# The last expert's weight in column halves, with the first output groups written by halves

## The chip, the core and the metric

The kernel runs on one core of one Trainium2 chip. The metric is the device time of one execution in microseconds, as the median of several runs. The kernel before takes 160.81 us (three runs, 159.79 to 162.02). The core has a matrix engine (TensorE, "PE" in the profile), a vector engine (VectorE, "DVE"), a scalar engine (ScalarE, "ACT"), GpSimd ("POOL"), and SyncE ("SP"), which in this kernel issues the output transfers. Sixteen DMA engines move data between memory and the core's SBUF.

## The reference, cut to what matters

Two operators run one after the other. The first is an attention in which each query sees six chunks of 32 keys, chosen by an upper bound on the chunk's scores; 4 batches, 8 heads, 768 positions, 64 columns a head. Its output, as a matrix x of 3072 rows and 512 columns, feeds a soft mixture of eight experts with four slots each:

```python
logits = x @ phi                       # 3072 x 32
d = softmax(logits, axis=0)            # over the rows
slot_input = (d.T @ x).reshape(8, 4, 512)
for e in range(8):
    h = np.maximum(slot_input[e] @ w1[e], 0.0)   # 4 x 1024
    slot_out[e] = h @ w2[e]                      # 4 x 512
c = softmax(logits, axis=1)            # over the slots
out = c @ slot_out.reshape(32, 512)    # 3072 x 512
```

Every row of the output needs every slot's output, so no row can be finished before the last expert's w2 has been used. But a column of the output needs only that column of each w2.

## The kernel before, in words

**The attention** works on 16 pairs of heads, p = 0 to 15, in one loop written out by hand (the schedule is manual: each engine runs its instructions in the order of the code). For each pair there are six units of scores (`UNITS`). `scores(p, u)` lets TensorE make the scores in PSUM and ScalarE take the exponential into an SBUF tile `ex`. `select(p, u)`, on GpSimd, sets the part above the diagonal of units 0 to 3 to zero, in place in `ex` (line 339). `pv_mm(p, u)` multiplies `ex` by the values (line 353); within a unit the block on the diagonal comes last. The units of one pair are spread over the loop: the products of units 0 and 1 come at the end of the pair's own turn, the others in the next turn.

**The loads** of keys, queries, values and weights are all issued from GpSimd's queue[...]. `load_w(i)` for i = 0 to 7 brings `w1` of an expert (line 115), for i = 8 to 15 its `w2` (line 121). The list `w_at` says in which turn which of them is issued; the last two, `w2` of experts 6 and 7, are issued at the end of the turn of pair 13. In GpSimd's order the next instructions are the four selections of pair 14, then the making of a small constant (`stack`), then the selections of pair 15. In the profile the tiles of `w2` are called w_0_97 to w_7_104, and the last one, w_7_104, is what the change is about. It is loaded in three pieces: the first four of its eight row groups (`to[:, 0]`, line 124), then two pieces of two groups each (line 127).

**After the last pair** TensorE sums up the slots (`slot_first`, `slot_last`), makes `h` for both groups of four experts (`h_mm`, line 692), transposes it (`turn_h`), and sums `h @ w2` into two PSUM tiles `so_ps[0]` and `so_ps[1]`, one for each half of 256 columns (`so_mm`, line 724): first experts 0 to 3, then 4 to 6 with the first half of the columns before the second, then expert 7 in the three pieces in which its weight lands. Each `so_mm` of expert 7 covers both halves of the columns.

**The output.** The two sums are copied to `so` in bf16 (lines 743 and 744, VectorE and ScalarE). Then 12 groups of 256 rows follow: two products each (`o_ps`, line 756), copied out by VectorE and ScalarE (line 757) to a tile `o_sb`, and sent by SyncE (lines 759 and 761). In the first group each row tile is sent alone; the others go out as 512 KB with 4 KB a partition. After the second group, `turn_c` and `take_c` (lines 763 and 764) prepare the weights `cT` of the last batch.

Of the kernel before, what the change touches and what calls it, by code (L numbers as in the profile page):

```python
# [9 lines left out]
F32 = mybir.dt.float32  # L10
BF16 = mybir.dt.bfloat16
# [19 lines left out]
def kernel(  # L31
# [10 lines left out]
    nc = tc.nc  # L42
    B, H, S, D = q.shape
# [3 lines left out]
    P = 128  # L47
    NT = S // P
# [5 lines left out]
    Dm, NS = moe_phi.shape  # L54
    E, _, F = moe_w1.shape
    SPE = NS // E
    NDG = Dm // P
    NFG = F // P
    FH = F // 2
    GH = FH // P  # L60
# [50 lines left out]
    w2_sb = [static.tile([P, NFG, Dm], BF16, name=f"w2_{e}") for e in range(E)]  # L111

    def load_w(i):
        if i < E:
            nc.gpsimd.dma_start(out=w1_sb[i], in_=moe_w1[i].rearrange("(g p) f -> p g f", p=P))
        else:

            to = w2_sb[i - E].rearrange("p (n g) d -> p n (g d)", n=2)
            rows = moe_w2[i - E].rearrange("(n p g) d -> p n (g d)", n=2, p=P)
            if i < 2 * E - 1:  # L120
                nc.gpsimd.dma_start(out=to, in_=rows)
            else:

                nc.gpsimd.dma_start(out=to[:, 0], in_=rows[:, 0])
                for c in range(0, GH * Dm, GH * Dm // 2):
                    z = c + GH * Dm // 2
                    nc.gpsimd.dma_start(out=to[:, 1, c:z], in_=rows[:, 1, c:z])

    load_k(0)
    load_q(0)  # L130
# [4 lines left out]
        out=ident, in_=ident, compare_op=ALU.not_equal, fill=1.0,  # L135
# [22 lines left out]
        out=ahead, in_=ahead, compare_op=ALU.is_ge, fill=NEG,  # L158
# [38 lines left out]
    cT = static.tile([P, B * S], BF16, name="cT")  # L197
# [259 lines left out]
    def turn_c(b, pool, tag):  # L457

        c = st.pop(("c", b))
        ps = pool.tile([P, NT, P], BF16, name="cT_ps", tag=tag)  # L460
        for t in range(NT):
            for g in range(2):
                nc.tensor.matmul(
                    ps[g * 2 * NS:(g + 1) * 2 * NS, t, :], lhsT=c[:, t], rhs=ident, is_transpose=True)
        st["cps", b] = ps

    def take_c(b):

        ps = st.pop(("cps", b)).rearrange("s (g t) (j i a) -> s t g i a j", t=2, i=2, a=PP)
        to = cT[:, b * S:(b + 1) * S].rearrange("s (g i t a j) -> s t g i a j", i=2, t=2, a=PP, j=NJ // 2)  # L470
        for t in range(2):
            nc.scalar.copy(to[:, t], ps[:, t])
# [16 lines left out]
    for j in range(NJ):  # L489
        for i in range(2):  # L490
            nc.tensor.matmul(
                k0_ps[j // (NJ // 2)][i * D:(i + 1) * D, j % (NJ // 2), :], lhsT=src[:, i, j, :],
                rhs=ident[:NP, :NP], is_transpose=True)
# [24 lines left out]
    bounds_min(1)  # L518
    blocks(1, nc.vector.tensor_mul)
    load_w(0)  # L520
    load_k(4)
    relu_q(1, lambda to, x: nc.gpsimd.tensor_scalar_max(to, x, 0.0))
# [6 lines left out]
    for p in range(NPAIR):  # L529
# [42 lines left out]
        if p == 0:  # L572
            load_w(1)
# [54 lines left out]
        for i in w_at[p]:  # L628
            load_w(i)
        if p == NPAIR - 2:  # L630
# [7 lines left out]
            for g in range(4):  # L638
                nc.gpsimd.affine_select(
                    out=stack, in_=stack, compare_op=ALU.not_equal, fill=1.0,  # L640
                    base=-g * NS, pattern=[[-1, NS]], channel_multiplier=1)
            e_all = static.tile([P, NS], F32, name="e_all")
            hT = [h_all[:, i] for i in range(2)]
# [6 lines left out]
    halves = ((0, NT // 2), (NT // 2, NT))  # L650
# [25 lines left out]
    moe = ctx.enter_context(tc.tile_pool(name="moe", bufs=2, reuse_waits="tile"))  # L676
    outp = ctx.enter_context(tc.tile_pool(name="outp", bufs=7, reuse_waits="tile"))
    ps_h = ctx.enter_context(tc.tile_pool(name="ps_h", bufs=4, space=bass.MemoryType.PSUM, reuse_waits="tile"))
    ps_o = ctx.enter_context(tc.tile_pool(name="ps_o", bufs=4, space=bass.MemoryType.PSUM, reuse_waits="tile"))
# [5 lines left out]
    DH = Dm // 2  # L685
# [17 lines left out]
    def turn_h(eg, f):  # L703
        h_sb = st["h", eg, f]
        hT_ps = ps_o.tile([P, GH, P + NS], BF16, name="hT_ps", tag="o")
        for fg in range(GH):
            nc.tensor.matmul(
                hT_ps[:, fg, :P], lhsT=h_sb.rearrange("p (c g) -> p g c", g=GH)[:, fg, :], rhs=ident, is_transpose=True)

        c = 4 * SPE * eg  # L710

        def own_slots(t):
            return t[:, :, c:c + 4 * step].rearrange("p f (g s) -> p f g s", s=step)[:, :, :, :SPE]

        nc.vector.tensor_copy(own_slots(hT[eg][:, f * GH:(f + 1) * GH]), own_slots(hT_ps))

    def so_mm(experts, rows, spread=False):

        units = [(e, fg, i) for i in range(2) for fg in rows for e in experts]
        if not spread:  # L720
            units = [(e, fg, i) for fg in rows for i in range(2) for e in experts]
        for n, (e, fg, i) in enumerate(units):
            g = n % 4
            nc.tensor.matmul(
                so_ps[i][32 * g:32 * (g + 1), :], lhsT=hT[e // 4][:, fg, 32 * (e % 4):32 * (e % 4 + 1)],
                rhs=w2_sb[e][:, fg, i * DH:(i + 1) * DH],
                start=(e < 4 and fg == 0), stop=(e == E - 1 and fg == NFG - 1), skip_group_check=True)

    h_mm(0, 0)
    h_mm(0, 1)  # L730
# [3 lines left out]
    turn_h(0, 1)  # L734
    turn_h(1, 0)
    so_ps = [ps_o.tile([P, DH], F32, name=f"so_ps{i}", tag="o") for i in range(2)]
    so_mm(range(4), range(NFG))
    turn_h(1, 1)
    so_mm(range(4, E - 1), range(NFG), True)
    for a, z in ((0, GH), (GH, GH + GH // 2), (GH + GH // 2, NFG)):  # L740
        so_mm((E - 1,), range(a, z), True)
    so = moe.tile([P, Dm], BF16, name="so")
    nc.vector.tensor_copy(so[:, :DH], so_ps[0])
    nc.scalar.copy(so[:, DH:], so_ps[1])


    for g in range(B * NT // 2):
        rows = out[2 * g * P:2 * (g + 1) * P, :].rearrange("(p i) d -> p i d", i=2)
        o_sb = outp.tile([P, 2, Dm], F32, name="o_sb", tag="o_sb")
        for i in range(2):  # L750
            n = 2 * g + i

            cuts = (0, DH, Dm) if n == 0 else (0, Dm)
            for m, (a, z) in enumerate(zip(cuts, cuts[1:])):
                o_ps = ps_o.tile([P, z - a], F32, name="o_ps", tag="o")
                nc.tensor.matmul(o_ps, lhsT=cT[:, n * P:(n + 1) * P], rhs=so[:, a:z])
                (nc.vector.tensor_copy if (i + m) % 2 == 0 else nc.scalar.copy)(o_sb[:, i, a:z], o_ps)  # L757
            if g == 0:
                nc.sync.dma_start(out=rows[:, i], in_=o_sb[:, i])
        if g > 0:  # L760
            nc.sync.dma_start(out=rows, in_=o_sb)
        if g == 1:
            turn_c(B - 1, ps_h, "h")
            take_c(B - 1)


# [28 lines left out]
```

The softmax here doesn't subtract the row's maximum and nothing guards it: scores larger than these inputs give would overflow.

## Time and profile before

| | |
|---|---|
| median, lowest and highest of 3 runs | 160.81, 159.79, 162.02 us |
| span of the profiled execution | 159.6 us |
| busy share of PE, DVE, ACT, POOL | 88%, 72%, 69%, 61% |
| mean granted clock of TensorE | 0.963 |
| loads (GpSimd's queue) | 26.25 MB as stored, in bf16 |
| output (SyncE's queue) | 6.29 MB |
| attention and slots on TensorE, up to | 130 us |
| h and the experts' sums | 130 to 140.2 us |
| output stream on the DMA engines | from about 142 to 158 us |

A line of the timeline reads: start in us, duration in us, engine, line of the code, operation, output and inputs; in square brackets stands how long the engine was idle before it, and what ended the wait. In the table of DMA issues the last column is the time from issue to landing. "PEclk" is the clock that TensorE was granted, in tenths of full speed.

### The profile page before, as it was taken

The page shows a single profiled execution, that of the slowest core. Times are in us where ns is not written, and L with a number is a line of the kernel's source. Part 1 is how long each engine was busy: PE and PEld are TensorE (multiplying, and loading weights), DVE is VectorE, ACT ScalarE, POOL GpSimd, SP SyncE. Part 2 cuts the span into 40 slices and gives each one's busy share as a digit, 9 for nine tenths or more (in the row PEclk, how much of TensorE's full clock was granted, in tenths as well). Part 3 has the DMA queues.
Part 4 walks back from the last instruction along what each step waited for, and adds up shares of the span by engine and source line. Part 5 has one row for each costly group of instructions (what it writes and reads, how often), then busy time and mean ns, then how long its engine had stood idle before and what let it go on. Part 6 is the DMA issues. An engine that isn't in the chain of part 4 may idle for free.

```text
span 159.6 us, 6240 instructions
## 1 busy us (share of the span) xinstructions
PE 140.3 (88%) x2644; PEld 92.5 (58%) x2644; DVE 114.5 (72%) x366; ACT 110.4 (69%) x145; POOL 97.2 (61%) x177
## 2 busy tenths in 40 slices
PE   6869889999999999999999999999999999878200
PEld 2346566767767776766767667665755866632000
DVE  3966987889898778998898698889449444069400
ACT  3256967789888877989896978979879522079300
POOL 6978799597878959597786859677656001000000
PEclk9986999999999999999999999999999999999955
DMA  2999999999999999999999999999999999439996
GB/s 38 158 179 193 210 193 209 184 183 163 191 188 210 196 207 195 211 193 208 199 185 208 198 211 196 209 197 215 205 206 215 215 215 210 87 118 407 404 408 241
DMA packets 40475, 32.93 MB, mean 206 GB/s; under 512 B 26368, under 2 KB 32512, under 8 KB 40448
## 3 DMA queue, kind: packets, MB, share of 16 engines
q0 software_dynamic: 38576, 26.25, 111.2%
q1 hardware_dynamic: 1872, 6.29, 10.0%
q8 instruction: 20, 0.33, 0.7%
q14 instruction: 7, 0.06, 0.1%
HBM read 52.49 MB, written 6.29 MB: 368 GB/s over the span
## 4 chain that ended last, share of the span: by engine, by line
PE 40%; DMA 28%; POOL 13%; issue 5%; ACT 3%; DVE 3%; POOLq 0%; DVEq 0%
DMA w_7_104<-in_moe_w_dram 16%; DMA w_2_99<-in_moe_w_dram 9%; PE sc_ps L315 9%; PE pv_ps L353 9%; PE sc_ps L322 6%; PE tr_ps L209 6%; DMA out_dram<-o_sb 3%; PE sc_ps L309 3%; PE ub_ps L274 3%; POOL k_bf L95 2%; POOL ex L339 2%; ACT o_sb L757 2%; POOL q_bf L95 2%; PE xT_ps L376 2%; PE ns_ps L292 1%
## 5 line engine op out<-in xcount | busy, mean ns | idle before, releaser
L330 ACT ACTIVATE ex<-sc_ps 128x1024 bf16<-128x1024 f32 x80 | 78.4, 1025 | 14.2 <-PE sc_ps L322 13.7
L339 POOL TENSOR_SCALAR_AFFINE_SELECT ex<-ex 128x256 bf16<-128x256 bf16 x64 | 32.3, 508 | 16.4 <-ACT ex L330 16.0
L315 PE MATMUL sc_ps<-qT,kT 64*128 64x512 bf16 (+3 forms) x256 | 35.3, 312 | 1.1 <-ACT ex L330 0.7
L322 PE MATMUL sc_ps<-nsT,smask 64*128 64x384 bf16 (+3 forms) x256 | 33.7, 299 | 0.0
L241 DVE TENSOR_REDUCE kmm<-kT 128x24 bf16<-128x768 bf16 x32 | 29.1, 942 | 0.1
L353 PEld LDWEIGHTS <-ex 128*128 128x128 bf16 x640 | 22.0, 97 | 8.0 <-issue 6.3
L315 PEld LDWEIGHTS <-kT 64*128 64x128 bf16 x256 | 13.0, 94 | 16.3 <-issue 5.9
L367 DVE TENSOR_TENSOR x_sb<-pv_ps,inv 128x768 bf16<-128x768 f32 (+1 forms) x17 | 15.4, 910 | 0.6
L322 PEld LDWEIGHTS <-smask 64*128 64x128 bf16 x256 | 13.1, 96 | 1.3
L220 DVE COPY qT<-tr_ps 128x768 bf16<-128x768 bf16 x14 | 7.8, 557 | 7.7 <-PE tr_ps L209 7.7
L215 ACT COPY kT<-tr_ps 128x768 bf16<-128x768 bf16 x14 | 11.3, 807 | 1.9 <-PE tr_ps L209 1.9
L95 POOL DMA_DIRECT2D k_bf<-in_k_dram x16 | 11.2, 698 | 0.8 <-POOLq L779 0.8
L298 DVE COPY nsT<-ns_ps 128x640 bf16<-128x640 bf16 x16 | 7.7, 481 | 3.8 <-PE ns_ps L292 3.8
L95 POOL DMA_DIRECT2D q_bf<-in_q_dram x16 | 10.4, 649 | 0.1
L209 PE MATMUL tr_ps<-ident,q_bf 96*64 96x96 bf16 x256 | 8.7, 212 | 1.5 <-ACT kT L215 0.9
L381 DVE COPY xT<-xT_ps 128x768 bf16<-128x768 bf16 (+1 forms) x16 | 8.5, 532 | 2.1 <-PE xT_ps L376 2.1
L309 PE MATMUL sc_ps<-ahead,ident 128*128 128x128 bf16 x64 | 9.1, 223 | 0.5 <-ACT ex L330 0.2
L274 PE MATMUL ub_ps<-bd,qp 128*128 128x48 bf16 x160 | 8.6, 183 | 0.6 <-ACT qp L504 0.6
L757 DVE COPY o_sb<-o_ps 128x512 f32<-128x512 f32 (+1 forms) x12 | 7.5, 665 | 2.1 <-DMA out_dram<-o_sb 1.0
L309 PEld LDWEIGHTS <-ident 128*128 128x128 bf16 x64 | 4.0, 97 | 8.2 <-issue 7.1
L260 POOL TENSOR_TENSOR bd<-kmm,own 128x96 bf16<-128x96 bf16 x14 | 4.8, 346 | 6.2 <-DVE kmm L241 6.1
L209 PEld LDWEIGHTS <-q_bf 96*64 96x64 bf16 x256 | 6.6, 111 | 3.1 <-issue 1.3
(191 smaller groups left out, 292.0 us busy)
## 6 DMA issues: line engine op xcount, KB each, us to landing
out_dram<-o_sb SPq DMA_DIRECT2D x11, 512.0 KB, 4.9
k_bf<-in_k_dram POOLq DMA_DIRECT2D x16, 192.0 KB, 9.1
q_bf<-in_q_dram POOLq DMA_DIRECT2D x16, 192.0 KB, 8.6
w_0_89<-in_moe_w_dram POOLq DMA_DIRECT2D x1, 1024.0 KB, 11.2
w_1_90<-in_moe_w_dram POOLq DMA_DIRECT2D x1, 1024.0 KB, 11.8
w_2_91<-in_moe_w_dram POOLq DMA_DIRECT2D x1, 1024.0 KB, 10.8
w_3_92<-in_moe_w_dram POOLq DMA_DIRECT2D x1, 1024.0 KB, 12.6
w_4_93<-in_moe_w_dram POOLq DMA_DIRECT2D x1, 1024.0 KB, 13.7
```

The costliest lines, as they stand in the source:

```text
L95: nc.gpsimd.dma_start(out=t, in_=src[b, h:h + 2].rearrange("h (p j) d -> p h (j d)", j=NJ))
L209: nc.tensor.matmul(ps[i * D:(i + 1) * D, j, :], lhsT=src[:, i, j, :], rhs=ident[:NP, :NP], is_transpose=True)
L215: copy(kT.rearrange("d (a j) -> d a j", j=NJ), st.pop(("tr", p, 0)).rearrange("d j a -> d a j"))
L241: nc.vector.tensor_reduce(st["kmm", p][:, s, 0, :], st["kT", p].rearrange("d (c i) -> d c i", i=CH), axis=AX.X, op=op)
L274: nc.tensor.matmul(ub_ps[:, t - 1], lhsT=x[:, t * P:(t + 1) * P], rhs=bd[:, s, :], start=False, stop=(s == 2), skip_group_check=True)
L309: nc.tensor.matmul(ps[:, i, c:c + P], lhsT=ident, rhs=ahead, start=first, stop=False, skip_group_check=True)
L315: nc.tensor.matmul(ps[:, i, c:c + w], lhsT=kT[r, kg * P:(kg + 1) * P], rhs=qT[r, q0:q0 + w], start=first and n == 0, stop=False, skip_grou ...
L322: nc.tensor.matmul(ps[:, i, c + lo - q0:c + w], lhsT=smask[r, kg, :], rhs=nsT[r, lo - P:q0 + w - P], start=False, stop=True, skip_group_ch ...
L330: nc.scalar.activation(ex[:, :, :width], ps[:, :, :width], func=ACT.Exp, scale=scale)
L339: nc.gpsimd.affine_select(out=d, in_=d, compare_op=ALU.is_ge, fill=0.0, base=0, pattern=[[0, 2], [1, NJ], [NJ, PP]], channel_multiplier=-1)
L353: nc.tensor.matmul(ps[:, i, t, :], lhsT=ex[:, i, o:o + P], rhs=vt[:, i, kg, :D + 1], start=(u == 0 and n == 0), stop=((u, kg) == last_of[t ...
L367: nc.vector.tensor_mul(st["x", b][:, t0:t1, h:h + 2, :].rearrange("p t i d -> p i t d"), ps[:, :, t0:t1, :D], inv[:, :, t0:t1].broadcast_t ...
```

## The change

The last expert's `w2` is loaded by halves of the columns instead of by row groups: four pieces, first columns 0 to 255 of the eight row groups (in two pieces of four groups), then columns 256 to 511. The sums of expert 7 for the first half of the columns are then done, copied to `so`, and used for the first three of four output groups, while the second half of the weight is still on its way. The first four groups of rows are written in two transfers each, one for each half of the columns, all eight with 1 KB a row. The remaining eight groups are as before, with whole rows. The last batch's `turn_c` and `take_c` come after the four groups instead of after the second one. `so_mm` is rewritten to take the half of the columns as an argument; the order of the sums of experts 0 to 6 stays the same.

The aim is to fill the time in which the DMA engines bring the end of the last weight and wait for the first output with output of the first half.

```diff
@@ load_w, the last expert
-                nc.gpsimd.dma_start(out=to[:, 0], in_=rows[:, 0])
-                for c in range(0, GH * Dm, GH * Dm // 2):
-                    z = c + GH * Dm // 2
-                    nc.gpsimd.dma_start(out=to[:, 1, c:z], in_=rows[:, 1, c:z])
+                for a in range(0, Dm, Dm // 2):
+                    for n in range(2):
+                        nc.gpsimd.dma_start(
+                            out=w2_sb[i - E][:, n * GH:(n + 1) * GH, a:a + Dm // 2],
+                            in_=rows[:, n].rearrange("p (g d) -> p g d", g=GH)[:, :, a:a + Dm // 2])
@@ the sums
-    def so_mm(experts, rows, spread=False):
...
+    def so_mm(experts, rows, halves=(0, 1)):
+        for n, (fg, e) in enumerate((fg, e) for fg in rows for e in experts):
             g = n % 4
+            for i in halves:
...
-    so_mm(range(4, E - 1), range(NFG), True)
-    for a, z in ((0, GH), (GH, GH + GH // 2), (GH + GH // 2, NFG)):
-        so_mm((E - 1,), range(a, z), True)
+    for i in range(2):
+        so_mm(range(4, E - 1), range(NFG), (i,))
@@ the output
+    NG = B * NT // 2
+    NB = 4
+    o_tiles = {}
+
+    def combine(g, a, z, pool, tag):
+        if g not in o_tiles:
+            o_tiles[g] = outp.tile([P, 2, Dm], F32, name="o_sb", tag="o_sb")
+        o_sb = o_tiles[g]
+        for i, copy in enumerate((nc.vector.tensor_copy, nc.scalar.copy)):
+            n = 2 * g + i
+            o_ps = pool.tile([P, z - a], F32, name="o_ps", tag=tag)
+            nc.tensor.matmul(o_ps, lhsT=cT[:, n * P:(n + 1) * P], rhs=so[:, a:z])
+            copy(o_sb[:, i, a:z], o_ps)
+        rows = out[2 * g * P:2 * (g + 1) * P, a:z].rearrange("(p i) d -> p i d", i=2)
+        nc.sync.dma_start(out=rows, in_=o_sb[:, :, a:z])
+
+    so_mm((E - 1,), range(NFG), (0,))
     nc.vector.tensor_copy(so[:, :DH], so_ps[0])
+    for g in range(NB - 1):
+        combine(g, 0, DH, ps_h, "h")
+    so_mm((E - 1,), range(NFG), (1,))
     nc.scalar.copy(so[:, DH:], so_ps[1])
...
+    combine(NB - 1, 0, DH, ps_h, "h")
+    for g in range(NB):
+        combine(g, DH, Dm, ps_o, "o")
+    turn_c(B - 1, ps_h, "h")
+    take_c(B - 1)
+    for g in range(NB, NG):
+        combine(g, 0, Dm, ps_o, "o")
```

More of the change, by code (lines that the diff above doesn't have):

```diff
@@ L715, in turn_h @@
         nc.vector.tensor_copy(own_slots(hT[eg][:, f * GH:(f + 1) * GH]), own_slots(hT_ps))
-    def so_mm(experts, rows, spread=False):
[L719 to L722, printed above, removed]
-            g = n % 4
[L724 to L727, printed above, removed]
+    def so_mm(experts, rows, halves=(0, 1)):
+        for n, (fg, e) in enumerate((fg, e) for fg in rows for e in experts):
+            g = n % 4
+            for i in halves:
+                nc.tensor.matmul(
+                    so_ps[i][32 * g:32 * (g + 1), :], lhsT=hT[e // 4][:, fg, 32 * (e % 4):32 * (e % 4 + 1)],
+                    rhs=w2_sb[e][:, fg, i * DH:(i + 1) * DH],
+                    start=(e < 4 and fg == 0), stop=(e == E - 1 and fg == NFG - 1), skip_group_check=True)
     h_mm(0, 0)
@@ L736 @@
     so_ps = [ps_o.tile([P, DH], F32, name=f"so_ps{i}", tag="o") for i in range(2)]
-    so_mm(range(4), range(NFG))
+    for fg in range(NFG):
+        for i in range(2):
+            so_mm(range(4), (fg,), (i,))
     turn_h(1, 1)
-    so_mm(range(4, E - 1), range(NFG), True)
-    for a, z in ((0, GH), (GH, GH + GH // 2), (GH + GH // 2, NFG)):
-        so_mm((E - 1,), range(a, z), True)
+    for i in range(2):
+        so_mm(range(4, E - 1), range(NFG), (i,))
     so = moe.tile([P, Dm], BF16, name="so")
+    NG = B * NT // 2
@@ L743 @@
+    so_mm((E - 1,), range(NFG), (0,))
     nc.vector.tensor_copy(so[:, :DH], so_ps[0])
+    for g in range(NB - 1):
+        combine(g, 0, DH, ps_h, "h")
+    so_mm((E - 1,), range(NFG), (1,))
     nc.scalar.copy(so[:, DH:], so_ps[1])
[L747 to L764, printed above, removed]
+    combine(NB - 1, 0, DH, ps_h, "h")
```

## The prediction, made before the result was known

> **What bounds the kernel now.** I read the page first, then the chain of waits, then GpSimd's queue in order of time, since the loads are issued there.
>
> ```profile
> PEclk9986999999999999999999999999999999999955
> DMA  2999999999999999999999999999999999439996
> GB/s 38 158 179 193 210 193 209 184 183 163 191 188 210 196 207 195 211 193 208 199 185 208 198 211 196 209 197 215 205 206 215 215 215 210 87 118 407 404 408 241
> ```
>
> Slices are 4 us. The DMA engines are full from the second slice to the 34th (inputs, counted in bf16), nearly idle in slices 35 and 36 (136 to 144 us), then full with the output at about 407 GB/s. The hole is what the change is aimed at. The chain of waits, in order of time, says what closes it:
>
> ```profile
> 114.30 25.52 DMA w_7_104<-in_moe_w_dram
> 139.82 0.04 issue
> 139.86 0.29 PE so_ps_3787 L724 x2
> ```
>
> The last piece of the last expert's w2 lands at 139.82; the first output transfer is issued at 141.48 (SyncE's first row in the timeline), so landing to issue is 1.6 us: the last sums, a cast of 0.42 (DVE so), a product, a copy. But TensorE had not waited long: the timeline has its sums of experts 4 to 6 until 138.24, and the list of waits gives the wait for w_7_104 as 0.99 us. From there the output is a plain stream:
>
> ```profile
> 138.00:140.00 2.00, 1.01 (x32) 0.63 (x24) 0.00 (x0) 0.00 (x0) 0.00 (x0) 1.00 0.18 34
> 140.00:142.00 2.00, 1.46 (x15) 0.67 (x13) 1.27 (x3) 1.26 (x4) 0.00 (x0) 1.00 0.00 0
> 142.00:158.00 16.00, 5.88 (x32) 2.02 (x28) 6.70 (x11) 6.76 (x13) 0.00 (x0) 0.78 0.99 393
> ```
>
> The columns end with granted clock, DMA share and GB/s. From 142 to 158 us 6.29 MB leave at 393 GB/s with the engines 0.99 busy: the end of the kernel is the time of the first output issue plus 18.1 us (159.6 - 141.48). Whatever moves that issue moves the end.
>
> Now the place where the loads are issued, GpSimd's queue, with the loads' times to landing:
>
> ```profile
> 97.89 1.07 POOL L107 DMA_DIRECT2D v_buf_87<-in_v_dram  x1
> 98.96 0.70 POOL L121 DMA_DIRECT2D w_2_99<-in_moe_w_dram  x1
> 99.65 0.73 POOL L121 DMA_DIRECT2D w_3_100<-in_moe_w_dram  x1
> ...
> 111.23 0.76 POOL L121 DMA_DIRECT2D w_6_103<-in_moe_w_dram  x1
> 111.99 0.57 POOL L124 DMA_DIRECT2D w_7_104<-in_moe_w_dram  x1
> 112.55 0.54 POOL L127 DMA_DIRECT2D w_7_104<-in_moe_w_dram  x1
> 114.30 0.53 POOL L127 DMA_DIRECT2D w_7_104<-in_moe_w_dram  x1 [1.20 <-DMA w_2_99<-in_moe_w_dram]
> 114.83 0.98 POOL L339 TENSOR_SCALAR_AFFINE_SELECT ex<-ex 128x256 bf16<-128x256 bf16 x2
> ```
>
> ```profile
> w_2_99<-in_moe_w_dram POOLq DMA_DIRECT2D x1, 1024.0 KB, 15.1
> w_3_100<-in_moe_w_dram POOLq DMA_DIRECT2D x1, 1024.0 KB, 19.2
> ```
>
> The third piece of w_7 waited 1.20 us for w_2_99, a transfer with which it shares no data. Counting issues back from it (w_7 twice, w_6, w_5, w_4, v, w_3, w_2), w_2 is the eighth before: a load here waits for the landing of the eighth load before it. So a fourth piece waits for w_3_100, which lands at 99.65 + 19.2 = 118.85 us. The changed program's instructions say the same: its fourth piece waits on the semaphore that w_3_100 counts on.
>
> **What the Trainium skill says.** "DMA: Bandwidth & Descriptors", section "Anatomy of one DMA — SWDGE (gpsimd) path": DMA engines do not wait on semaphores, the issuing sequencer does, before dispatch. The trace agrees: the 1.20 us are idle time of GpSimd. "TensorE: Matmul & The Clock Gate", section "Architectural detail": GpSimd takes its instructions strictly in order, so what stands behind a waiting load waits too; the trace shows the two selections starting at 114.83, the moment the third piece is issued. The same page, section "Part 1: The HAM clock gate": after an idle window of about 3.4 us the clock is halved, and it takes such a window of work to come back. The trace agrees in kind: the PEclk row falls to 5 after TensorE's last work at 148.6, and near 11 us after a thin stretch:
>
> ```profile
> 7.70:11.10 3.40, 1.89 (x43) 1.27 (x43) 2.03 (x15) 2.07 (x3) 3.37 (x5) 1.00 1.51 174
> 147.90:151.30 3.40, 0.71 (x3) 0.10 (x1) 1.38 (x2) 1.24 (x3) 0.00 (x0) 0.96 1.02 405
> ```
>
> **The change, part by part.** (1) Four pieces of w_7 instead of three, each of 512 runs. A load of 512 runs (w1) took GpSimd 0.76 us, pieces of 128 runs 0.53 to 0.57. After w_6 ends at 111.99: first piece to 112.75, second to 113.51, third as before from 114.30 (after w_2) to 115.06. The fourth waits for w_3: 118.85, plus 0.28 us that w_2's landing (98.96 + 15.05 = 114.02) left to the restart at 114.30, is 119.13; issued by 119.89. Behind it stand the four diagonal selections of pair 14. The first two, at 114.83 to 115.81 before, now end at 120.39 and 120.87. Who waits for them: TensorE's pv_mm(14, 0) and pv_mm(14, 1), in place on the same ex tiles, whose diagonal block comes last. Before, these 16 matmuls ran from 117.74 to 118.40, with about 2.4 us to spare; now the last can't end before about 120.95. TensorE is in order, and pair 15's scores follow, so ScalarE's next exponential (119.52, itself waiting 0.91 us for TensorE) moves too. Shift: 120.95 - 118.40 = 2.55 us. Nothing hides it: from 118.4 to 124.4 TensorE is 5.71 of 6.00 us busy, and slot sums, h, and the experts' sums follow in one chain.
>
> (2) The stall leaves TensorE idle for about 2.3 us, so the clock may be halved for about 3.4 us in pair 15. That costs between 0 (no fall, or only ScalarE's pace counts) and 1.7 us (all of 3.4 us at half speed is on the path). I take 0.8, the middle.
>
> (3) Smaller rows of the load: 512 B instead of 2 to 4 KB on the SBUF side. In the window from 16 to 114 us, which mixes in k, q and v with rows of 1 KB down to 128 B, the engines moved 199 GB/s, against 215 in slices of weights alone; on 1 MB that is 4.9 against 5.3 us, at most 0.4 later. It is hidden: TensorE now reaches this expert only at 140.8.
>
> (4) The first half's sums, cast and three groups go ahead of the second half. Sums of experts 4 to 6 end at 138.24 + 2.55 = 140.79; the first issue follows after the first four sums of the last expert's half (0.11) and the same 1.62 us of sum, cast, product and copy (139.86 to 141.48): 142.52. That is 1.04 us later than before, 1.84 with the clock. The second half, landed by about 140.2, is waited for by nobody.
>
> (5) Eight half-width output transfers instead of four full ones: 2.1 MB in rows of 1 KB rather than 4 KB. No row shows this; the bounds are 0 and, by the 8% of (3) on 5.2 us, 0.4. I take 0.35. The 8 + 8 half copies (0.42 and 0.46 us a pair side by side) keep ahead of a 256 KB transfer, which takes 0.65 us at 400 GB/s; the later turn_c hides behind that queue.
>
> Sum: 1.04 + 0.8 + 0.35 = 2.2 us; 160.8 + 2.2 = 163.0 us.
>
> **The rivals.** (A) The wait stands as worked out but the clock stays up, because the idle stretch falls across two windows: 160.8 + 1.04 + 0.35 = 162.2. For it: 137.6 to 141.0 us holds a similar hole and the clock stayed. (B) The clock is down for its whole 3.4 us on the path: 160.8 + 1.04 + 1.7 + 0.4 = 163.9, and over 164 if w_3 lands a little later or the slow clock also stretches the slot sums. (C) The wait is hidden or short: then TensorE takes the first half at 138.24, the first issue is at 138.24 + 0.11 + 1.62 = 139.97, 1.5 earlier, less 0.35: 159.7 us, faster than before. For it: the DMA hole of 136 to 142 us is real and half the expert would be in by about 137.5. Against it: w_3's landing follows from a queue that is full from 4 us on, and the selections' slack is only 2.4 of the 5.1 us by which they move.
>
> **How the numbers follow.** Forecast 0.40, A 0.20, B 0.26, C 0.14. A and most of the forecast lie within 2% (157.6 to 164.0). B sits on the upper bound: two thirds of it and a quarter of the forecast (the runs of the kernel before spread from 159.8 to 162.0) pass it, about 0.28. C passes the lower one in 0.04 at most. The range leaves out C and the far end of B: 160.6 to 164.9.
>
> **What would show it.** Right: the fourth piece of w_7 idle some 4 us before it, released by w_3_100; the next selection near 120 us; an idle stretch of TensorE at pv_ps released by GpSimd; no wait for w_7_104 at the last sums; first output issue at 142.5 to 143.3; perhaps a 5 in the PEclk row near 122 us. Wrong: if the fourth piece does not wait, or pv_ps does not, the end comes at 159 to 160; if the output stream runs well under 390 GB/s in its first 5 us, step 5 is too small.

## The result, and the profile after

The changed kernel takes 165.23 us (median of 6 runs, 164.24 to 167.14) against 160.81 us: slower, by a ratio of 1.0267 (95% interval 1.0203 to 1.0331), some 4.3 us. The medians are of all executions; the ratios here and below leave out those more than 1.5% above the fastest of the same kernel. The profiled executions have spans of 163.4 and 159.6 us. The one of the kernel before was long for it: it took 161.43 us, and the seven executions of the same kernel beside the first experiments have a median span of 158.6 us. So a moment read against its trace makes a changed version look better than it is, by up to 1 us. The page of the changed kernel:

```profile
PEclk9987999999999999999999999999978999999955
DMA  2999999999999999999999999999999999069993
GB/s 39 156 163 191 211 193 210 183 188 178 187 198 205 195 213 189 211 196 206 188 196 207 204 201 202 200 214 216 194 217 216 212 197 141 5 233 354 409 404 144
...
q8 instruction: 21, 0.34, 0.8%
```

The hole in the DMA row, which the change was to fill, is still there, and it is empty now: 5 GB/s in the 35th slice, where the kernel before had 87 and 118 GB/s in the 35th and 36th. Two things are new: a dip of PEclk ahead of it (the 7 and the 8), and a slice of 354 GB/s at the start of the output. The last line counts the fetches of instructions by the DMA engines; before, it read 20.

GpSimd's queue in the changed kernel, in order of time:

```profile
111.25 0.76 POOL L121 DMA_DIRECT2D w_6_103<-in_moe_w_dram  x1
112.01 2.27 POOL L126 DMA_DIRECT2D w_7_104<-in_moe_w_dram  x3
117.90 0.74 POOL L126 DMA_DIRECT2D w_7_104<-in_moe_w_dram  x1 [3.63 <-DMA w_3_100<-in_moe_w_dram]
118.65 1.89 POOL L340 TENSOR_SCALAR_AFFINE_SELECT ex<-ex 128x256 bf16<-128x256 bf16 x4
```

The fourth piece of the last weight waits 3.63 us for w_3_100, and pair 14's selections stand behind it: 118.65 instead of 114.83. Who waits for them, from the timeline of TensorE and VectorE:

```profile
117.76 0.35 PE L354 MATMUL pv_ps<-v_buf_87,ex 128*128 128x65 bf16 x6
...
119.22 0.69 PE L354 MATMUL pv_ps<-v_buf_87,ex 128*128 128x65 bf16 x10 [1.11 <-POOL ex L340]
119.85 0.61 PE L406 MATMUL si_ps<-x_sb,e 128*32 128x512 bf16 x6
...
132.85 0.23 DVE L440 CAST siT<-siT_ps_3617 128x64 bf16<-128x64 f32 x1
```

TensorE stood idle for 1.11 us until the selections came. The product si_ps (of the slot weights and x), which follows the waiting products, starts at 119.85 instead of 118.33: 1.52 us late. The last cast of the slot sums (siT) ends at 133.08 instead of 130.03: 3.05 us late. So half of the delay comes after the wait. Busy time by stage shows what is different there; the number behind POOL's is the granted clock. First the changed kernel, then the kernel before:

```profile
118.00:122.00 4.00, 2.85 (x32) 1.26 (x28) 1.28 (x2) 1.26 (x3) 3.45 (x10) 0.81 1.14 215
122.00:124.00 2.00, 2.00 (x28) 1.57 (x28) 0.73 (x2) 1.30 (x2) 1.02 (x2) 0.53 1.06 213
```

```profile
118.00:122.00 4.00, 3.81 (x66) 2.20 (x62) 2.77 (x6) 3.09 (x5) 1.81 (x6) 1.00 1.19 212
122.00:124.00 2.00, 1.90 (x29) 1.05 (x28) 1.71 (x4) 1.95 (x3) 1.80 (x4) 1.00 1.06 213
```

Then the output of the changed kernel: SyncE's first issue, and the stages of its stream (last columns: DMA share and GB/s).

```profile
143.01 14.57 SPq L760 DMA_DIRECT2D out_dram<-o_sb  x16
```

```profile
142.00:144.00 2.00, 1.57 (x16) 0.81 (x16) 1.33 (x5) 1.22 (x4) 0.00 (x0) 1.00 0.00 0
144.00:144.50 0.50, 0.35 (x4) 0.26 (x3) 0.42 (x1) 0.48 (x2) 0.00 (x0) 1.00 0.36 129
...
145.00:146.00 1.00, 0.94 (x16) 0.65 (x15) 0.92 (x3) 0.81 (x4) 0.00 (x0) 1.00 1.02 341
...
147.00:148.00 1.00, 0.87 (x4) 0.29 (x3) 1.00 (x3) 1.00 (x3) 0.00 (x0) 1.00 0.99 344
...
160.50:161.00 0.50, 0.00 (x0) 0.00 (x0) 0.00 (x0) 0.00 (x0) 0.00 (x0) 0.50 0.43 164
161.00:161.50 0.50, 0.00 (x0) 0.00 (x0) 0.00 (x0) 0.00 (x0) 0.00 (x0) 0.50 0.06 25
161.50:162.00 0.50, 0.00 (x0) 0.00 (x0) 0.00 (x0) 0.00 (x0) 0.00 (x0) 0.50 0.08 33
```

The kernel before, at the start of its stream, in the middle of it and at its end:

```profile
142.50:143.00 0.50, 0.50 (x4) 0.26 (x3) 0.30 (x1) 0.50 (x3) 0.00 (x0) 1.00 1.01 381
144.00:145.00 1.00, 0.82 (x4) 0.28 (x3) 1.00 (x2) 1.00 (x3) 0.00 (x0) 1.00 1.01 401
157.50:158.00 0.50, 0.00 (x0) 0.00 (x0) 0.00 (x0) 0.00 (x0) 0.00 (x0) 0.50 0.86 336
```

While the half-width transfers leave, the DMA engines of the changed kernel are as busy as ever (share 0.99 to 1.02 in the lines shown) and move 341 to 344 GB/s, where the kernel before shows 401: the stream is fed, it is slower in itself. And at its end there is a tail of about 1.2 us at a share of 0.06 to 0.08, and 0.06 is 1/16: a single DMA engine is late. The kernel before ends without such a tail.

The account between the two spans, each from these views: first output issue 143.01 against 141.48, +1.5 us; issue to first byte about 1.3 against 0.9, +0.4 (129 of some 345 GB/s in the half microsecond from 144.0 puts the first byte at 144.3; 102 of 402 from 142.0 puts it at 142.4 before); slow rows, +0.85 (first byte to where the bulk ends: 16.4 against 15.55); the late engine, +1.25. That is 4.0 for a difference of 3.8. Between the times of many executions the difference is 4.3, since the traced execution of the kernel before was a long one.

### The profile page after: what moved, and what is told of

Read it like the earlier page. It is cut to its first block, busy times and chain, and to the rows that moved or that the text cites. A ratio compares the mean times of both kernels' runs of the same rounds, so it can differ in the third digit from the quotient of the medians.

```text
span 163.4 us, 6275 instructions
## 1 busy us (share of the span) xinstructions
PE 142.3 (87%) x2651; PEld 93.7 (57%) x2651; DVE 115.9 (71%) x370; ACT 111.0 (68%) x148; POOL 98.5 (60%) x178
## 4 chain that ended last, share of the span: by engine, by line
PE 71%; ACT 10%; DMA 6%; issue 4%; DVE 2%; POOL 1%; ACTq 0%; DVEq 0%; POOLq 0%
PE pv_ps L354 14%; PE sc_ps L316 14%; PE sc_ps L323 9%; PE tr_ps L210 9%; ACT ex L331 5%; PE ub_ps L275 4%; PE sc_ps L310 4%; DMA out_dram<-o_sb 3%; PE xT_ps L377 3%; PE ns_ps L293 3%; DMA q_bf<-in_q_dram 3%; PE h_ps L693 2%; ACT o_sb L758 2%; PE lg_ps L391 1%; PE so_ps_3788 L723 1%
## 5 line engine op out<-in xcount | busy, mean ns | idle before, releaser
L323 PE MATMUL sc_ps<-nsT,smask 64*128 64x384 bf16 (+3 forms) x256 | 34.2, 304 | 0.0
L316 PEld LDWEIGHTS <-kT 64*128 64x128 bf16 x256 | 13.0, 95 | 16.4 <-issue 6.2
L758 ACT COPY o_sb<-o_ps 128x256 f32<-128x256 f32 (+1 forms) x16 | 7.3, 483 | 9.5 <-PE o_ps L757 6.5
L758 DVE COPY o_sb<-o_ps 128x256 f32<-128x256 f32 (+1 forms) x16 | 8.4, 555 | 4.2 <-DMA out_dram<-o_sb 2.4
L757 PE MATMUL o_ps<-so,cT 128*128 128x256 bf16 (+1 forms) x32 | 7.2, 325 | 3.8 <-ACT o_sb L758 2.9
```

The source lines that it names most:

```text
L316: nc.tensor.matmul(ps[:, i, c:c + w], lhsT=kT[r, kg * P:(kg + 1) * P], rhs=qT[r, q0:q0 + w], start=first and n == 0, stop=False, skip_grou ...
L323: nc.tensor.matmul(ps[:, i, c + lo - q0:c + w], lhsT=smask[r, kg, :], rhs=nsT[r, lo - P:q0 + w - P], start=False, stop=True, skip_group_ch ...
L758: copy(o_sb[:, i, a:z], o_ps)
```

## The experiments

My theory at this point: four separate costs, namely the wait on GpSimd, the clock halved after it, the narrow output rows, and a DMA engine held up by one more fetch of instructions. The rivals: that the wait alone brought all of it, or that the output alone did, the wait being hidden.

### The fourth piece issued after the selections

```diff
-                for a in range(0, Dm, Dm // 2):
-                    for n in range(2):
-                        (piece a, n)
+                for a, n in ((0, 0), (0, 1), (Dm // 2, 0)):
+                    last_piece(a, n)
...
         select(p, 3)
+        if p == NPAIR - 2:
+            last_piece(Dm // 2, 1)
```

> The changed kernel, with one edit: the fourth piece of the last weight is issued after the four selections of pair 14 instead of ahead of them. Theory (the gap is made of a wait on GpSimd that holds the selections, a slow TensorE clock after it, slower 1 KB rows, and one extra fetch of instructions in the output stream): no wait for pv_ps on GpSimd, clock at 1.0, TensorE done with experts 4 to 6 near 138.2 us, first output issue near 140.0; the output stream stays slow (1.3 us for rows and issue, 1.3 us for one late DMA engine), so 161.8 us, 3.4 less than the changed kernel. Rival 1 (the wait was harmless, the loss is all in the output): 165 us, as the changed kernel. Rival 2 (all the loss came from the wait, slow output included): 159.7 us.

Measured: 161.55 us against 160.26 beside it on the same chip, 1.0067 (1.0033 to 1.0101). The timeline of its GpSimd:

```profile
113.43 0.74 POOL L115 DMA_DIRECT2D w<-in_moe_w_dram  x1 [0.38 <-DMA w<-in_moe_w_dram]
114.18 1.05 POOL L343 TENSOR_SCALAR_AFFINE_SELECT ex<-ex 128x256 bf16<-128x256 bf16 x2
...
116.89 0.51 POOL L343 TENSOR_SCALAR_AFFINE_SELECT ex<-ex 128x256 bf16<-128x256 bf16 x1 [0.41 <-ACT ex L334]
118.35 0.76 POOL L115 DMA_DIRECT2D w<-in_moe_w_dram  x1 [0.94 <-DMA w<-in_moe_w_dram]
```

The same piece is issued at about the same time, still behind a wait, but the selections of pair 14 are done by then, and TensorE's list of waits has none for GpSimd. The stages of this run:

```profile
118.00:122.00 4.00, 3.81 (x62) 2.20 (x58) 3.17 (x7) 3.09 (x5) 3.09 (x9) 1.00 1.11 215
142.00:144.00 2.00, 1.86 (x19) 0.86 (x18) 1.59 (x4) 1.91 (x6) 0.00 (x0) 1.00 1.00 344
158.00:158.50 0.50, 0.00 (x0) 0.00 (x0) 0.00 (x0) 0.00 (x0) 0.00 (x0) 0.50 0.06 25
```

The clock stays at 1.00 from 118 to 124 us, the slot sums end at 129.60, and the first output is issued at 139.54, 1.9 us before that of the kernel before in its long trace, so by estimate (less the 1.0 us by which that trace is long) some 0.9 us before it in a usual execution. The second half of the weight was in time. So the purpose of the change is reached here, and the kernel is still slower than before: the output eats it (343 to 344 GB/s from 142 to 146 us, 21 fetches, a tail of 25 and 8 GB/s from 158 us). Both rivals fall: without the wait three quarters of the loss are gone (ratio 1.0067 against 1.0267), and neither part is all of it.

### The wait alone, in the kernel before

```diff
-                nc.gpsimd.dma_start(out=to[:, 0], in_=rows[:, 0])
-                for c in range(0, GH * Dm, GH * Dm // 2):
-                    z = c + GH * Dm // 2
-                    nc.gpsimd.dma_start(out=to[:, 1, c:z], in_=rows[:, 1, c:z])
+                for n in range(2):
+                    for c in range(0, GH * Dm, GH * Dm // 2):
+                        z = c + GH * Dm // 2
+                        nc.gpsimd.dma_start(out=to[:, n, c:z], in_=rows[:, n, c:z])
```

> The kernel before, with one edit: the last weight comes in four pieces by row groups instead of three, everything else as it was. Theory: the fourth piece waits some 3.6 us for the load of expert 3's second weight, the selections of pair 14 end near 119.6 us, TensorE's clock falls, the sums of experts 4 to 6 end 3.0 us later (141.3 instead of 138.2), the last sums 1.8 us later than 139.9, so 162.6 us. Rival 1 (the wait is hidden by the wait for the last landing, 139.8): 160.8 us, as before. If the clock stays up: 161.1 us.

Measured: 162.54 us, 1.0129 (1.0094 to 1.0164). The theory had 162.6; as a difference it had 1.8 us, and the ratio gives 2.1. So a fourth piece costs 2 us with nothing else changed:

```profile
118.15 0.53 POOL L127 DMA_DIRECT2D w<-in_moe_w_dram  x1 [4.79 <-DMA w<-in_moe_w_dram]
118.68 1.89 POOL L339 TENSOR_SCALAR_AFFINE_SELECT ex<-ex 128x256 bf16<-128x256 bf16 x4
...
119.26 0.75 PE L353 MATMUL pv_ps<-v_buf,ex 128*128 128x65 bf16 x10 [1.88 <-POOL ex L339]
```

```profile
118.00:122.00 4.00, 2.74 (x24) 1.21 (x26) 0.77 (x2) 0.06 (x1) 3.33 (x10) 0.68 1.10 217
```

TensorE's products waited 1.88 us for the selections, its clock was 0.68 from 118 to 122 us, and the first output was issued at 143.07, though the weights were in well before: the DMA share was 0.03 from 138.3 to 140 us and 0.00 from 140 to 142. The narrow rows and the late engine are absent, and their costs with them.

### Narrow output rows alone, in the kernel before

```diff
-            if g == 0:
-                nc.sync.dma_start(out=rows[:, i], in_=o_sb[:, i])
-        if g > 0:
-            nc.sync.dma_start(out=rows, in_=o_sb)
+        if g < 4:
+            for a in (0, DH):
+                nc.sync.dma_start(out=rows[:, :, a:a + DH], in_=o_sb[:, :, a:a + DH])
+        else:
+            nc.sync.dma_start(out=rows, in_=o_sb)
```

> The kernel before, with one edit: each of the first four groups of output is sent in two transfers, one for each half of the columns (1 KB rows), after the same copies; no other engine's instructions change. Theory: 2.1 MB leave at about 345 instead of 405 GB/s, 0.85 us more, and 0.4 us more from the first issue to the first byte: 162.1 us, all 16 DMA engines ending together. Rival 1 (rows of 1 KB are as good, the changed kernel's stream was not fed fast enough): 160.8 us. Rival 2 (small rows also make one DMA engine late): 163.3 us, with a tail of 0.06 DMA share.

Measured: 162.08 us (three executions of 161.66 to 162.25, one of 164.18), 1.0094 (1.0055 to 1.0133). From the stages of its span:

```profile
144.00:146.00 2.00, 1.63 (x8) 0.58 (x7) 1.75 (x3) 1.75 (x4) 0.00 (x0) 1.00 1.02 342
158.50:159.00 0.50, 0.00 (x0) 0.00 (x0) 0.00 (x0) 0.00 (x0) 0.00 (x0) 0.50 0.91 352
159.00:159.50 0.50, 0.00 (x0) 0.00 (x0) 0.00 (x0) 0.00 (x0) 0.00 (x0) 0.50 0.03 8
```

342 GB/s at a share of 1.02, and no tail: the rows of 1 KB are slow here too, behind the products and copies of the kernel before, and they do not make one engine late. Rival 1 and rival 2 fall. The transfers are smaller as well, 256 KB instead of 512 KB, and no run changes only that. But the first two transfers of the kernel before have 256 KB too, with rows of 2 KB, and they ran at 381 GB/s (142.50 to 143.00 above): the narrower row goes with the lower rate at the same size.

### A longer program alone, in the kernel before

```diff
+    pad = ps_h.tile([P, 64], F32, name="pad", tag="h")
+    for _ in range(7):
+        nc.tensor.matmul(pad, lhsT=w_rhs[:, :P], rhs=w_rhs[:, :64])
```

These lines stand after the last product, where TensorE is idle.

> The kernel before, with one edit: seven small matmuls (64 columns) on a loaded weight after the last product, when TensorE has nothing left to do; 14 more instructions of TensorE, as many as the changed kernel has. Their sums are not used. Theory: a 21st fetch of instructions falls into the output stream, one of 16 DMA engines ends 1.2 us after the others, 162.0 us. Rival (the late engine in the changed kernel has another cause): 20 fetches, 160.8 us.

Measured: 162.38 us, 1.0123 (1.0077 to 1.0169). The count of fetches on the page, their count from 142 us on, and the end of the stream:

```profile
q8 instruction: 21, 0.34, 0.8%
```

```profile
q8 instruction: 1, 0.02, 0.3%
```

```profile
157.00:158.00 1.00, 0.00 (x0) 0.00 (x0) 0.00 (x0) 0.00 (x0) 0.00 (x0) 0.50 0.58 225
158.00:158.50 0.50, 0.00 (x0) 0.00 (x0) 0.00 (x0) 0.00 (x0) 0.00 (x0) 0.50 0.08 33
158.50:159.00 0.50, 0.00 (x0) 0.00 (x0) 0.00 (x0) 0.00 (x0) 0.00 (x0) 0.50 0.06 25
```

Seven matmuls that delay nobody on TensorE cost 2.0 us (by the interval 1.2 to 2.7): the 14 instructions bring one more fetch, it falls into the output stream, and one DMA engine ends last, alone. In the kernel before, no fetch comes after 138 us. The trace does not name the engines, so that the late one is the one that carried the fetch is inferred; of the nine traces here, the four with 21 fetches have the last of them inside the output stream, and the other five have none there. The theory had 1.2 us; in this trace first issue to end of span takes 19.6 us instead of 18.1, 1.5 more, and whether the rest is more than scatter these runs don't tell. The changed kernel has 14 more instructions of TensorE too: seven more products, each with a load of weights.

### TensorE kept busy during the wait

```diff
+        if p == NPAIR - 2:
+            keep_warm(6, w1_sb[0][:, 0, :512], ps_m, "m")
         pv_mm(p, 0)
         pv_mm(p, 1)
```

> The changed kernel, with one edit: six matmuls of 512 columns on a loaded weight just ahead of the products of pair 14's units 0 and 1, to keep TensorE busy (1.3 us) while it waits for the selections; their sums are not used. Theory (of the 3.0 us by which TensorE comes late, 1.5 are the wait itself and 1.5 the clock halved after it): granted clock 1.0 from 118 to 124 us, slot sums about 1.5 us earlier than in the changed kernel, 3.2 us above the kernel before instead of 4.4. Rival (the late slot sums come from ScalarE's pace, the clock does not matter): as the changed kernel, 4.4 us above before. If the filler only adds to the wait: 5 us above.

Measured: 164.08 us (163.70 to 165.43), 1.022 (1.0163 to 1.0278): 3.6 us above before, between the theory and its rival; by the time alone this is inconclusive. The trace answers the part on the clock. Its profiled execution was the slowest of the four, and the fourth piece waited longer in it (5.46 us, until 119.89), but TensorE's clock held, although TensorE was idle for 1.62 us after the filler:

```profile
118.00:122.00 4.00, 2.28 (x27) 1.29 (x28) 0.00 (x0) 0.82 (x2) 2.10 (x4) 1.00 1.19 210
122.00:124.00 2.00, 2.00 (x38) 1.20 (x33) 1.29 (x2) 0.96 (x2) 1.45 (x7) 1.00 1.07 217
```

From the start of si_ps to the end of siT it took 11.72 us (121.84 to 133.56); the kernel before takes 11.70, the changed one 13.23. The other traces say the same: in all seven in which the clock held, this stretch takes 11.7 us, and in the two in which it fell 13.23 and 12.99 (the four pieces in the kernel before). So the halved clock is worth 1.3 to 1.5 us here, and the rival, ScalarE's pace, falls. What the filler saves is uncertain in the time, because the length of the wait differs from run to run: the fourth piece restarted at 117.90, 118.15 and 119.89 in the three traces that have the wait ahead of the selections.

### Two groups by halves, with the late fourth piece

```diff
-    NB = 4
+    NB = 2
...
-    for g in range(NB - 1):
+    for g in range(NB):
         combine(g, 0, DH, ps_h, "h")
     so_mm((E - 1,), range(NFG), (1,))
     nc.scalar.copy(so[:, DH:], so_ps[1])
-    combine(NB - 1, 0, DH, ps_h, "h")
```

> The late fourth piece, and only the first two groups of rows written by halves instead of four (both ahead of the second half's sums); TensorE has 4 matmuls fewer than the changed kernel, 3 more than before. Theory: first output byte 1.5 us earlier than in the kernel before, 1.0 MB in slow rows costs 0.44 us; with the 21st fetch of instructions (1.3 us) about 160.5, without it 159.2 us, where before is 160.3. Rival (the gap cannot be filled, the stream only starts earlier and stalls): 161.5 us, as with four groups.

Measured: 160.24 us against 160.48, 0.9977 (0.9950 to 1.0004), from 22 runs of it and 43 of the kernel before. Its page has 20 fetches:

```profile
q8 instruction: 20, 0.33, 0.8%
```

The profiled span is 158.5 us, and the engines end together near 157 us. With the wait out of the way, half of the slow rows and no late engine, the idea is level with the kernel before, at best 0.5% faster: about 0.8 us less than the theory had hoped for. The theory had its first byte "1.5 us earlier" from the long trace of the kernel before, which can account for what is missing; no run shows that it does. It is the best version found, and not clearly better than the kernel before.

### The same with fewer warming matmuls at the start

```diff
-    keep_warm(4, zeros)
+    keep_warm(1, zeros)
```

> As the one with two groups, and three warming matmuls of the start fewer, so that TensorE has as many instructions as in the kernel before. Theory: 20 fetches of instructions, all 16 DMA engines end together, 159.2 us, 1 us below the kernel before. Rival (the fetch is bound to the place in time and not to the number of instructions): one engine late again, 160.5 us. If the three warming matmuls were needed, the start is slower and the gain is lost.

Measured: 161.07 us, 1.0005 (0.9977 to 1.0034). It has 20 fetches, but so had the version before it, so it tells nothing on them. The hoped-for gain is not there, and the interval overlaps that of the version before it, so the times do not tell the two apart. Its profiled execution (162.25 us) was one of its longer ones: its clock is 0.53, 0.50 and 0.50 in the three stages from 10 to 16 us. But the kernel before, with all four warming matmuls, has a dip there as well (0.77, 0.50 and 0.87). That the missing matmuls made the start slower, the last branch of the expectation, is therefore not shown.

## Why the prediction was wrong, point by point

The direction and the mechanism of the wait were right, the cost of the output was not: forecast 163.0 us, range to 164.9, measured 165.23. Two numbers of each trace show where the time went:

| trace | first output issue, us | from there to the end of the span, us |
|---|---|---|
| the kernel before | 141.48 | 18.1 |
| the changed kernel | 143.01 | 20.4 |
| late fourth piece | 139.54 | 20.4 |
| four pieces, in the kernel before | 143.07 | 18.1 |
| narrow rows, in the kernel before | 141.25 | 19.2 |
| longer program, in the kernel before | 141.06 | 19.6 |
| two groups by halves, late piece | 139.72 | 18.8 |

The prediction took the second column as fixed but for 0.35 us.

**Step 1, the wait.** Right in kind: fourth piece, w_3_100, selections, pv_ps, in that order. It was put at 2.55 us on TensorE, some 2.3 of them idle, and measured 1.52, of them 1.11 idle, because w_3_100 landed at about 117.7 (the fourth piece restarted at 117.90) and not at 118.85. A landing behind a deep queue was read off one trace as if it were fixed; over the traces here the restart of that piece moves by 2 us.

**Step 2, the clock.** Put at 0.8, the middle of 0 to 1.7; measured 1.53, near the upper end: nearly all of the half clock fell on the path. Steps 1 and 2 together were put at 3.35 and measured 3.05: the errors cancel, which is luck. "TensorE: Matmul & The Clock Gate", section "Part 1: The HAM clock gate", has the clock halved after an idle window of about 3.4 us. The trace agrees with the size of the fall and its length (0.81 over 4 us and 0.53 over 2 us make 3.4 us at half clock), but not with what went before: TensorE was idle for 1.11 us and busy for 2.15 us of the 3.41 us ahead of the fall. The measurement decides, and it gives no simple rule either: from 137.6 to 141.0 us in the kernel before TensorE was busy for only 1.90 us, and the clock stayed.

**Step 3, the smaller rows of the load.** Right: the DMA share is 0.27 from 138 to 140 us and 0.00 from 140 to 142, so all of the weight was in before TensorE asked for its second half, and the timeline shows no wait for it at the last sums.

**Step 4, the first issue.** Forecast 142.5, or 143.3 with the clock; measured 143.01. It is as good as steps 1 and 2 together, by the same luck.

**Step 5, the output by halves: this is the step that failed.** It stood in the sum with 0.35 us, between 0 and 0.4, the upper bound being the loss of the loads with small rows. Measured in the changed kernel's trace: 0.85 us for the rows, 0.4 for the later first byte, 1.25 for the late engine, 2.5 in all (2.3 in the table, which counts to the end of the span and not to the last byte). The loads' loss was no bound for stores. The prediction's own sign of this came: the stream ran well under 390 GB/s in its first 5 us. "DMA: Bandwidth & Descriptors", section "Specifications", gives 512 B as the least transfer for full line rate; rows of 1 KB ran at 342 GB/s here, alone in the kernel before, against 401 and more, so the measurement decides. The fetch of instructions was not in the working at all, although the list of queues showed it: 20 packets, 0.33 MB, that is 16 KB each, by DMA engines that the output would need.

**The rivals.** (A), the clock staying up, and (C), the wait hidden, did not happen. The run with the late fourth piece comes close to (C): its first issue of 139.97 is near the 139.54 measured there, but its end of 159.7 is not, since the output was under-priced there too (161.55). The hole that it counted on was also read too wide: from 136 to 138 us the DMA engines of the kernel before still have a share of 0.59, so "nearly idle" holds only for the time after 138 us. (B) was nearest with 163.9, for its clock, and under-priced step 5 in the same way. The 0.28 for slower by over 2% was too low for the same reason.

## What to carry to other kernels

Splitting a load costs more than its descriptors: look up which earlier transfer the extra issue must wait for, and what stands behind it on the issuing engine. Where a kernel ends in a DMA stream with all engines busy, the width of a row and anything else that uses even one of the DMA engines can be on the path; hiding a wait ahead of the stream is worth nothing if it is paid for in the stream. Test the parts of such a change each alone in the old kernel: here three of them cost 1.5 to 2.1 us each, and the gain was eaten before it showed.

## What the runs showed of the hardware that I had not expected

Stores of 1 KB rows from SBUF ran at 341 to 346 GB/s with the engines fully busy, those with 4 KB a partition at about 400 to 410. With one more fetch of 16 KB of instructions in the midst of a full output stream, the stream ended about 1.2 us later on one DMA engine alone (share 0.06). An idle stretch of 1.11 us on TensorE, in a thin stretch of work, was followed by about 3.4 us at half clock, worth 1.5 us; one of 1.62 us, with filler matmuls ahead of it, was not. The time at which a load lands behind a queue of some 18 us moved by up to 2 us between runs.
